# A spectral filter and a gated MLP on one core: the forward 47-point stage of the later batches with x stationary, and its result turned by transposing DMAs

## The chip, the core and the metric

The kernel runs on 1 core of one Trainium2 chip. The metric is device time in microseconds (us), from launch to end. All engines of the core work at once on their own instruction queues and meet through semaphores: PE (TensorE, matmuls; PEld are its weight loads), DVE (VectorE), ACT (ScalarE), POOL (GpSimd) and SP (SyncE, which here only issues DMAs).

## The reference

```python
def _attn_ref(x, filt_r, filt_i):              # x: 8 batches x 3008 x 256
    X = np.fft.rfft(x, axis=1)
    F = (filt_r + 1j * filt_i)[None, :, :]     # 1505 x 256
    return np.fft.irfft(X * F, n=x.shape[1], axis=1)

def _moe_ref(x, w_in, w_out, beta):            # 24064 tokens, 256 -> 2048 -> 256
    h = x @ w_in
    g = h * (1.0 / (1.0 + np.exp(-beta * h)))
    return g @ w_out
```

The output of the first is reshaped to 8 * 3008 = 24064 tokens and goes into the second. Inputs and output are float32; the kernel multiplies in bfloat16.

## The kernel before, in words

**The transform.** 3008 = 47 * 64. A token's index in its batch is 32 p + j with p = 0..93 and j = 0..31, and p = 2 n1 + q. The forward transform has two stages. Stage 1 (`s1`) is a 47-point transform over n1: a contraction over the 94 values of p with the table `t1` of 94 x 96, whose 96 columns are 24 frequencies k1 x 2 parts (real, imaginary) x 2 values of q. Stage 2 (`s2`) contracts, for each k1, over the 128 values of (part, q, j) with the table `t2`. So between the stages the data has to turn: stage 1 gives (k1, part, q) per j, and stage 2 needs (part, q, j) on the partitions per k1. After stage 2 DVE multiplies by the filter (L603, L604, L607), POOL adds the halves (L608, `yh`), and two inverse stages follow: `s3` (L619) with `t3` and `s4` (L641) with `t4`, with a turn through DRAM (`d2`) between them. `s4` writes `y`, which has the 256 channels on the partitions.

**Batch 0** is done ahead of the main loop with everything on chip, in functions of its own (`s1_0`, `a0_turn` and so on); there stage 1 already has x stationary and its result is turned by PE. It is not touched.

**Batches 1 to 7** are done inside the main loop. The loop has 752 steps: 47 blocks of 512 tokens by 16 blocks of 128 hidden units. A step does two matmuls of 512 columns for the hidden layer (L782), the swish on ACT (L791), and, two steps later, four matmuls of 256 columns into the block's accumulators (L800). Every 16 steps a block is finished, DVE copies it from PSUM (`ost<-acc`, tile pool `ostp` with 2 buffers), and SP stores it (`out_block`, L759 and L761).

**The order is written by hand.** `at(s, fn, ...)` puts a piece of the transform of a later batch behind the hidden layer of step s. `first_step[b]` is 0, 80, 176, 272 and so on, some 96 steps a batch; in the code o is `first_step[b - 1]`, the step at which the tokens of batch b - 1 begin to enter the MLP; in the steps that follow, `s2`, `s3` and `s4` of batch b are done. `s23_steps` places `s2` and `s3`, `s4_steps` places `s4`, `s1_steps` places the 16 units of stage 1 of the next batch: for batch 2 at steps 54 to 76, for each batch b + 1 above at o + 7, o + 13, o + 23 and so on to o + 76. So batch 3 begins stage 1 at step 87. The planned steps:

```python
at(o + 80, a2_load, 2, g)         # batch 2, o = 0; batch 1 has o + 16
at(o + 82, a2_load, b + 1, g)     # batches 3 to 7
```

**Stage 1 before.** A unit `s1(b, i)` is one matmul (L573): `t1` is the stationary operand (96 columns), and x, two values of j by 256 channels, 512 columns, is the moving one. The result of 96 partitions x 512 is cast into a tile `a1` (pool `apool`, 4 buffers, one tile for each 8 values of j), by DVE, in batch 1 by ACT in 5 of 16 units. After four units `a1_store` (L356) stores the tile in the DRAM scratch `d1`. `a2_load` (L581) reads `d1` back in the turned order, in 4 groups of 6 frequencies, into `a2` tiles (pool `a2pool`, 5 buffers). The data of one batch, 1.5 MB, thus goes to DRAM and back.

PSUM tiles of all these pieces come from one pool, `fpsum`, of 3 buffers. x of the later batches is loaded by POOL's DMA queue in chunks of 8 values of j (`load_x`, pool `xpool` of 4 buffers); a chunk serves four units of `s1`. [...]

Of the kernel before, what the change touches and what calls it, by code (L numbers as in the profile page):

```python
# [10 lines left out]
P = 128  # L11
# [5 lines left out]
BF16 = mybir.dt.bfloat16  # L17
# [7 lines left out]
NK = 24  # L25
J = 32
KG = 6
JG = 8
# [8 lines left out]
def kernel(  # L37
# [10 lines left out]
    nc = tc.nc  # L48

    B, S, D = x.shape  # L50
# [5 lines left out]
    NDC = D // P  # L56
    NFB = FF // P
    NP = 2 * N1
    KP = 4 * NK
# [11 lines left out]
    tw = dict(reuse_waits="tile")  # L71
    dpool = ctx.enter_context(tc.tile_pool(name="dram_scratch", bufs=2, space=bass.MemoryType.DRAM))
# [20 lines left out]
    t1 = consts.tile([NP, KP], BF16, name="t1", tag="t1")  # L93
# [10 lines left out]
    xg = {}  # L104
    ys = {}
    st = {}

    def evac(dst, src, on_act, scale=None):
        if on_act:
            nc.scalar.activation(dst, src, ACT.Copy, scale=1.0 if scale is None else scale)  # L110
        elif scale is None:
            nc.vector.tensor_copy(dst, src)  # L112
        else:
            nc.vector.tensor_scalar_mul(dst, src, scale)  # L114
# [129 lines left out]
    MG = 4  # L244
# [100 lines left out]

    r_sq.close()

    def d_tiles(b):
        st["d1", b] = dpool.tile([NK, P, D], BF16, name="d1", tag="d1")
        st["d2", b] = dpool.tile([NK, P, D], BF16, name="d2", tag="d2")  # L350

    def a1_store(b, g):
        if g == 0:
            d_tiles(b)
        rows = st["d1", b].rearrange("k (a j) d -> (k a) j d", j=J)
        nc.sync.dma_start(rows[:, g * JG : (g + 1) * JG, :], st["a1", b][:])  # L356

    wst = ctx.enter_context(tc.tile_pool(name="wstage", bufs=2, **tw))
    zzpool = ctx.enter_context(tc.tile_pool(name="zzpool", bufs=4, **tw))
    WG = 4  # L360
# [169 lines left out]
    def tail_tile(i, shape, dt=F32):  # L530
        return pair[i].tile(shape, dt, name="pt", tag=f"pt{i}")
# [10 lines left out]
    for e in range(NDC):  # L542
        for h in range(2):
            ps = tail_tile(2 - e, [P, 4, P])
# [9 lines left out]
    r_sr.close()  # L554
    right.close()

    apool = ctx.enter_context(tc.tile_pool(name="apool", bufs=4, **tw))
    hpsum = ctx.enter_context(tc.tile_pool(name="hpsum", bufs=2, space=bass.MemoryType.PSUM, **tw))
    opsum = ctx.enter_context(tc.tile_pool(name="opsum", bufs=3, space=bass.MemoryType.PSUM, **tw))
    fpsum = ctx.enter_context(tc.tile_pool(name="fpsum", bufs=3, space=bass.MemoryType.PSUM, **tw))  # L560
# [5 lines left out]
    ostp = ctx.enter_context(tc.tile_pool(name="ostp", bufs=2, **tw))  # L566

    def s1(b, i, on_act):
        g, jj = divmod(2 * i, JG)
        if jj == 0:  # L570
            st["a1", b] = apool.tile([KP, JG, D], BF16, name="a1", tag="a1")
        ps = fpsum.tile([P, 512], F32, name="ps1", tag="f")
        nc.tensor.matmul(  # L573
            ps[:KP], lhsT=t1[:], rhs=xg[b, g][:NP, jj : jj + 2, :], start=True, stop=True
        )
        evac(st["a1", b][:, jj : jj + 2, :], ps[:KP], on_act)

    def a2_load(b, h):
        cols = st["d1", b].rearrange("k m d -> m k d")
        t = a2pool.tile([P, KG, D], BF16, name="a2", tag="a2")  # L580
        nc.sync.dma_start(t[:], cols[:, h * KG : (h + 1) * KG, :])  # L581
        st["a2", b, h] = t

    def s2_matmuls(b, i):
# [25 lines left out]

    def s3(b, i, on_act):
        g, kk = divmod(2 * i, KG)
        if ("z", b, g) not in st:
            st["z", b, g] = [zpool.tile([P, KG, D], BF16, name="z", tag="z"), 0]
        z = st["z", b, g]
        yh = st.pop(("yh", b, i))
        ps = fpsum.tile([P, 2, D], F32, name="ps3", tag="f")
        for e in range(2):
            nc.tensor.matmul(  # L619
                ps[:, e, :], lhsT=t3[:, 2 * i + e, :P], rhs=yh[:, e, :], start=True, stop=True  # L620
            )
        evac(z[0][:, kk : kk + 2, :], ps[:], on_act)
        z[1] += 2
        if z[1] == KG:
            cols = st["d2", b].rearrange("k m d -> m k d")
            nc.sync.dma_start(cols[:, g * KG : (g + 1) * KG, :], z[0][:])
# [36 lines left out]
    def at(s, fn, *a):  # L663
        plan.setdefault(int(s), []).append((fn, a))

    def s1_steps(b, units_, steps, act, on_act=()):
        assert len(steps) == len(units_)
        for i, s in zip(units_, steps):
            at(s, s1, b, i, i in on_act)
            if i % 4 == 3:  # L670
                at(s, a1_store, b, i // 4)

    def s23_steps(b, steps, lag, act):
        assert len(steps) == NU
        for i, s in enumerate(steps):
            at(s, s2, b, i)
            at(s + lag, s3, b, i, i % act == act - 1 if act else False)
# [6 lines left out]
    for b in range(1, B):  # L684
        o = first_step[b - 1]
        if b == 1:
            at(0, z_late, 1, 0)
            at(1, z_late, 1, 1)
            s1_steps(1, range(16), [3 + (2 * i + 1) // 3 for i in range(16)], False, (1, 4, 7, 10, 13))
            for i, r in enumerate((2, 3, 4, 5)):  # L690
                at(r, f_late, 1, i // 2, i % 2)
            for g in range(NG):
                at(o + 16, a2_load, 1, g)
# [12 lines left out]
            if B > 2:  # L706
                for g in range(4):
                    at(o + 24 + 3 * g, load_x, 2, g)
                late = (54, 55, 56, 57, 58, 59, 60, 61, 66, 67, 68, 70, 72, 73, 74, 76)
                s1_steps(2, range(16), [o + r for r in late], False)  # L710
                for g in range(NG):
                    at(o + 80, a2_load, 2, g)
                if B > 3:
                    for g in range(4):
                        at(o + (62, 68, 88, 92)[g], load_x, 3, g)
# [8 lines left out]
        if b + 1 < B:  # L724
            early = [o + 16 * n + s for n in range(4) for s in (7, 13)]
            late = [o + s for s in (66, 67, 69, 70, 72, 73, 75, 76)]
            s1_steps(b + 1, range(16), early + late, False)
            for g in range(NG):
                at(o + 82, a2_load, b + 1, g)
            if b + 2 < B:  # L730
                for g in range(4):
                    at(o + (30, 62, 88, 92)[g], load_x, b + 2, g)
# [6 lines left out]
    for s in range(NSTEP):  # L739
        i, fb = divmod(s, NFB)  # L740
# [31 lines left out]
    for s in range(NSTEP + 4):  # L772
        if s < NSTEP:
            i, fb = divmod(s, NFB)
# [3 lines left out]
            while pos < t0 + TB:  # L778
                b, n0 = divmod(pos, S)
                ln = min(S - n0, t0 + TB - pos)  # L780
                for dc in range(NDC):
                    nc.tensor.matmul(  # L782
                        hps[:, pos - t0 : pos - t0 + ln],
                        lhsT=win_sb[:, dc, fb * P : (fb + 1) * P],
                        rhs=ys[b][:, dc, n0 : n0 + ln],
                        start=(dc == 0),
                        stop=(dc == NDC - 1),
# [10 lines left out]
        for i, fb, tb in outs.get(s, ()):  # L798
# [3 lines left out]
                lhsT=blk[i * NFB + fb][:, tb * P : (tb + 1) * P],  # L802
                rhs=wout_sb[:, fb, :],
                start=(fb == 0 and (tb % 2 == 0 or lone)),
                stop=(fb == NFB - 1),
# [35 lines left out]
```

## Time and profile before

| | |
|---|---|
| Median of 3 runs | 780.7 us (780.31 to 780.71) |
| Profiled execution: its time, its span | 780.71 us, 778.9 us |
| Busy: PE, ACT, DVE, POOL | 768.9, 552.7, 447.1, 150.9 us |
| Granted TensorE clock | 1.00 |
| Stores of a1 to d1 (L356) | 28 of 384 KB, 5.4 us from issue to landing |
| Loads of a2 from d1 (L581) | 28 of 384 KB, 5.2 us |
| Stage 1 matmuls (L573) | 112, 41.9 us busy |
| DVE casts of stage 1 | 107, 686 ns each |
| ACT casts of stage 1 | 5, 581 ns each |

How to read it: the span is the time from the first to the last instruction of one profiled execution, and its own time is 1.8 us above the span. Matmuls overlap, so that the mean duration of one contains its latency; what one costs in a stream is read from the distance of two starts. Lines such as L573 are lines of the kernel before; in the changed kernel the same lines of code have other numbers.

### The profile page before, as it was taken

Reading aid. Unit: us, or ns where it says so; the run is one execution under the profiler, and the core shown is the slowest. Engines: PE = TensorE matmul, PEld = TensorE weight load, DVE = VectorE, ACT = ScalarE, POOL = GpSimd, SP = SyncE. Lnnn points to the kernel's source line nnn. Section 1 sums busy time; section 2 is a strip of 40 time slices with the busy share of each in tenths; the row PEclk is TensorE's granted clock in tenths of the full one; section 3 lists DMA queues with packets and bytes.
Section 4 is the critical chain, followed back from the end, with each engine's and each line's share of the span. In section 5 each row is a group of like instructions: output and inputs, shape, how many; then the busy total and the mean of one; then the engine's idle time right before and its main releaser. Section 6 shows DMA issues by size and latency. Waiting matters only on the chain.

```text
span 778.9 us, 15241 instructions
## 1 busy us (share of the span) xinstructions
PE 768.9 (99%) x6048; PEld 543.7 (70%) x6048; DVE 447.1 (57%) x716; ACT 552.7 (71%) x813; POOL 150.9 (19%) x154
## 2 busy tenths in 40 slices
PE   8899999999999999999999999999999999999997
PEld 5667667666776667866678666776667766676665
DVE  8878754766556665566546665567655666321001
ACT  7767877666677766777667776677666777777776
POOL 6714300312012210122201322022200222000000
PEclk9999999999999999999999999999999999999999
DMA  9967485244813358042671417622164111500101
GB/s 201 210 194 165 135 216 149 74 109 112 244 48 84 100 123 235 29 114 70 152 207 45 120 48 179 179 75 68 49 189 134 50 48 48 157 28 28 55 28 55
DMA packets 84411, 88.71 MB, mean 114 GB/s; under 512 B 5788, under 2 KB 74652, under 8 KB 84340
## 3 DMA queue, kind: packets, MB, share of 16 engines
q1 hardware_dynamic: 77940, 74.20, 31.5%
q0 software_dynamic: 4192, 13.40, 10.5%
q8 instruction: 47, 0.77, 0.4%
q10 hardware_dynamic: 2208, 0.14, 0.2%
q14 instruction: 24, 0.20, 0.1%
HBM read 54.47 MB, written 46.66 MB: 130 GB/s over the span
## 4 chain that ended last, share of the span: by engine, by line
PE 96%; ACT 1%; DVE 1%; issue 0%; POOL 0%; DVEq 0%; POOLq 0%
PE acc L800 42%; PE hps L782 42%; PE ps L573 3%; PE ps L641 2%; PE ps L589 2%; PE ps L619 2%; PE sps L454 0%; PE tp L403 0%; ACT aT L110 0%; ACT t L110 0%; ACT y L110 0%; DVE pq_t L440 0%; PE ps L408 0%; DVE u L226 0%; PE sps L433 0%
## 5 line engine op out<-in xcount | busy, mean ns | idle before, releaser
L791 ACT ACTIVATE gT<-hps,beta_sb 128x512 bf16<-128x512 f32 x752 | 516.6, 687 | 213.7 <-PE hps L782 212.9
L800 PE MATMUL acc<-wout_sb,gT 128*128 128x256 bf16 x3008 | 453.1, 272 | 0.0
L782 PE MATMUL hps<-y,win_sb 128*128 128x512 bf16 (+7 forms) x1728 | 447.8, 351 | 0.1
L800 PEld LDWEIGHTS <-gT 128*128 128x128 bf16 x3008 | 286.7, 98 | 121.7 <-issue 1.2
L608 POOL TENSOR_TENSOR yh<-a_t,b_t 128x512 bf16<-128x512 f32 x84 | 106.4, 1267 | 422.5 <-DVE b_t L607 422.1
L782 PEld LDWEIGHTS <-win_sb 128*128 128x128 bf16 x1728 | 164.7, 98 | 24.4 <-DVE y L114 0.3
L112 DVE COPY ost<-acc 128x512 f32<-128x512 f32 (+1 forms) x94 | 60.0, 679 | 138.2 <-PE acc L800 138.2
L112 DVE CAST a<-ps 96x512 bf16<-96x512 f32 x107 | 73.0, 686 | 52.2 <-PE ps L573 51.4
L114 DVE TENSOR_SCALAR y<-ps 128x376 bf16<-128x376 f32 (+2 forms) x128 | 63.2, 509 | 61.5 <-PE ps L641 57.9
L603 DVE TENSOR_TENSOR a_t<-ps,fr_sb 128x512 f32<-128x512 f32 x84 | 58.1, 692 | 67.5 <-PE ps L589 67.0
L604 DVE SCALAR_TENSOR_TENSOR b_t<-ps,fi_sb 64x512 f32<-64x512 f32 x84 | 58.2, 693 | 1.1
L607 DVE TENSOR_TENSOR b_t<-ps,fi_sb 64x512 f32<-64x512 f32 x84 | 57.4, 684 | 1.1
L112 DVE CAST z<-ps 128x512 bf16<-128x512 f32 x72 | 49.3, 685 | 1.7 <-PE ps L619 0.8
L641 PEld LDWEIGHTS <-zz 96*128 96x128 bf16 x448 | 29.7, 97 | 22.9
L573 PE MATMUL ps<-xg,t 94*96 94x512 bf16 x112 | 41.9, 381 | 0.0
L641 PE MATMUL ps<-t,zz 96*128 96x94 bf16 x448 | 34.7, 205 | 0.0
L589 PE MATMUL ps<-a,t 128*128 128x256 bf16 x168 | 32.1, 273 | 0.0
L619 PE MATMUL ps<-yh,t 128*128 128x256 bf16 x168 | 32.1, 273 | 0.0
L619 PEld LDWEIGHTS <-t 128*128 128x128 bf16 x168 | 16.2, 98 | 17.7 <-issue 0.6
L589 PEld LDWEIGHTS <-t 128*128 128x128 bf16 x168 | 16.1, 98 | 16.1
L171 POOL DMA_DIRECT2D xg<-in_x_dram x24 | 12.5, 524 | 56.7 <-PE ps L573 56.7
L573 PEld LDWEIGHTS <-t 94*96 94x96 bf16 x112 | 13.8, 123 | 10.4
(95 smaller groups left out, 177.8 us busy)
## 6 DMA issues: line engine op xcount, KB each, us to landing
out_dram<-ost SPq DMA_DIRECT2D x42, 512.0 KB, 3.0
d<-a SPq DMA_DIRECT2D x28, 384.0 KB, 5.4
a<-d SPq DMA_DIRECT2D x28, 384.0 KB, 5.2
d<-z SPq DMA_DIRECT2D x28, 384.0 KB, 3.7
zz<-d SPq DMA_DIRECT2D x28, 384.0 KB, 6.9
xg<-in_x_dram POOLq DMA_DIRECT2D x24, 384.0 KB, 6.1
out_dram<-ost SPq DMA_DIRECT2D x9, 256.0 KB, 5.5
ws<-in_moe_w_out_dram SPq DMA_DIRECT2D x4, 512.0 KB, 8.9
```

The lines of the kernel that those rows point to most:

```text
L112: nc.vector.tensor_copy(dst, src)
L114: nc.vector.tensor_scalar_mul(dst, src, scale)
L573: nc.tensor.matmul(ps[:KP], lhsT=t1[:], rhs=xg[b, g][:NP, jj : jj + 2, :], start=True, stop=True)
L589: nc.tensor.matmul(ps[:, e, :], lhsT=t2[:, k0 + e, :], rhs=st["a2", b, g][:, kk + e, :], start=True, stop=True,)
L603: nc.vector.tensor_tensor(a_t[:], ps[:], fr_sb[:, ks, :], ALU.mult)
L604: nc.vector.scalar_tensor_tensor(b_t[:M], ps[M:], -1.0, fi_sb[M:, ks, :], ALU.mult, ALU.mult)
L608: nc.gpsimd.tensor_tensor(yh[:], a_t[:], b_t[:], ALU.add)
L619: nc.tensor.matmul(ps[:, e, :], lhsT=t3[:, 2 * i + e, :P], rhs=yh[:, e, :], start=True, stop=True)
L641: nc.tensor.matmul(ps[:, e, :NP], lhsT=zz[:, j0 % JG + e, dc * P : (dc + 1) * P], rhs=t4[:], start=True, stop=True,)
L782: nc.tensor.matmul(hps[:, pos - t0 : pos - t0 + ln], lhsT=win_sb[:, dc, fb * P : (fb + 1) * P], rhs=ys[b][:, dc, n0 : n0 + ln], start=(dc ...
L791: nc.scalar.activation(gT[:], hps[:], ACT.Silu, scale=beta_sb[:, fb : fb + 1])
L800: nc.tensor.matmul(acc_of(i, tb)[:, tb % 2, :], lhsT=blk[i * NFB + fb][:, tb * P : (tb + 1) * P], rhs=wout_sb[:, fb, :], start=(fb == 0 an ...
```

## The change

For batches 1 to 7, stage 1 takes x as the stationary operand. A unit has four matmuls, one for each of four values of j: the stationary operand is x of 94 values of p by 128 channels, the moving one is `t1` with 96 columns. The result has 128 channels on the partitions and 4 x 96 columns, and its cast, still on the same engine and at the same step, writes it with permuted columns into one tile `a1` for the whole batch, of 128 partitions by 2 (channel halves) x 96 x 32. `apool` has 1 buffer. There are still 16 units: 8 groups of j by 2 channel halves.

`a1_store` and the scratch `d1` are gone. `a2_load` issues, in each of its 4 groups, two transposing DMAs on SP (8 a batch), each of which takes 128 partitions by 768 columns (6 frequencies x 4 x 32) of `a1` and writes 6 blocks of 128 x 128, transposed, into the same `a2` tile as before. The steps at which the units and `a2_load` stand are unchanged. The scratch `d2` of the inverse turn stays; its allocation moves into `s3`. Stage 2 and all that follows are as before.

```diff
--- before.py
+++ after.py
@@ -345,16 +345,6 @@
 
     r_sq.close()
 
-    def d_tiles(b):
-        st["d1", b] = dpool.tile([NK, P, D], BF16, name="d1", tag="d1")
-        st["d2", b] = dpool.tile([NK, P, D], BF16, name="d2", tag="d2")
-
-    def a1_store(b, g):
-        if g == 0:
-            d_tiles(b)
-        rows = st["d1", b].rearrange("k (a j) d -> (k a) j d", j=J)
-        nc.sync.dma_start(rows[:, g * JG : (g + 1) * JG, :], st["a1", b][:])
-
     wst = ctx.enter_context(tc.tile_pool(name="wstage", bufs=2, **tw))
     zzpool = ctx.enter_context(tc.tile_pool(name="zzpool", bufs=4, **tw))
     WG = 4
@@ -554,7 +544,7 @@
     r_sr.close()
     right.close()
 
-    apool = ctx.enter_context(tc.tile_pool(name="apool", bufs=4, **tw))
+    apool = ctx.enter_context(tc.tile_pool(name="apool", bufs=1, **tw))
     hpsum = ctx.enter_context(tc.tile_pool(name="hpsum", bufs=2, space=bass.MemoryType.PSUM, **tw))
     opsum = ctx.enter_context(tc.tile_pool(name="opsum", bufs=3, space=bass.MemoryType.PSUM, **tw))
     fpsum = ctx.enter_context(tc.tile_pool(name="fpsum", bufs=3, space=bass.MemoryType.PSUM, **tw))
@@ -566,19 +556,32 @@
     ostp = ctx.enter_context(tc.tile_pool(name="ostp", bufs=2, **tw))
 
     def s1(b, i, on_act):
-        g, jj = divmod(2 * i, JG)
-        if jj == 0:
-            st["a1", b] = apool.tile([KP, JG, D], BF16, name="a1", tag="a1")
+        jq, e = divmod(i, NDC)
+        if i == 0:
+            st["a1", b] = apool.tile([P, NDC, KP, J], BF16, name="a1", tag="a1")
         ps = fpsum.tile([P, 512], F32, name="ps1", tag="f")
-        nc.tensor.matmul(
-            ps[:KP], lhsT=t1[:], rhs=xg[b, g][:NP, jj : jj + 2, :], start=True, stop=True
-        )
-        evac(st["a1", b][:, jj : jj + 2, :], ps[:KP], on_act)
+        g, m0 = divmod(jq * MG, JG)
+        for m in range(MG):
+            nc.tensor.matmul(
+                ps[:, m * KP : (m + 1) * KP],
+                lhsT=xg[b, g][:NP, m0 + m, e * P : (e + 1) * P],
+                rhs=t1[:],
+                start=True,
+                stop=True,
+            )
+        evac(
+            st["a1", b][:, e, :, jq * MG : (jq + 1) * MG],
+            ps[:, : MG * KP].rearrange("p (m k) -> p k m", k=KP),
+            on_act,
+        )
 
     def a2_load(b, h):
-        cols = st["d1", b].rearrange("k m d -> m k d")
         t = a2pool.tile([P, KG, D], BF16, name="a2", tag="a2")
-        nc.sync.dma_start(t[:], cols[:, h * KG : (h + 1) * KG, :])
+        for e in range(NDC):
+            nc.sync.dma_start_transpose(
+                t[:, :, e * P : (e + 1) * P],
+                st["a1", b][:, e, 4 * KG * h : 4 * KG * (h + 1), :].rearrange("p k j -> p (k j)"),
+            )
         st["a2", b, h] = t
 
     def s2_matmuls(b, i):
@@ -610,6 +613,8 @@
 
     def s3(b, i, on_act):
         g, kk = divmod(2 * i, KG)
+        if i == 0:
+            st["d2", b] = dpool.tile([NK, P, D], BF16, name="d2", tag="d2")
         if ("z", b, g) not in st:
             st["z", b, g] = [zpool.tile([P, KG, D], BF16, name="z", tag="z"), 0]
         z = st["z", b, g]
@@ -667,8 +672,6 @@
         assert len(steps) == len(units_)
         for i, s in zip(units_, steps):
             at(s, s1, b, i, i in on_act)
-            if i % 4 == 3:
-                at(s, a1_store, b, i // 4)
 
     def s23_steps(b, steps, lag, act):
         assert len(steps) == NU
```

## The prediction

> **What bounds the kernel now.** First the page's busy times, then the chain of work that ended last: both name TensorE.
>
> ```profile
> PE 768.9 (99%) x6048; PEld 543.7 (70%) x6048; DVE 447.1 (57%) x716; ACT 552.7 (71%) x813; POOL 150.9 (19%) x154
> ...
> PE 96%; ACT 1%; DVE 1%; issue 0%; POOL 0%; DVEq 0%; POOLq 0%
> PE acc L800 42%; PE hps L782 42%; PE ps L573 3%; PE ps L641 2%; PE ps L589 2%; PE ps L619 2%; PE sps L454 0%; PE tp L403 0%; ACT aT L110 0%; ACT t L110 0%; ACT y L110 0%; DVE pq_t L440 0%; PE ps L408 0%; DVE u L226 0%; PE sps L433 0%
> ```
>
> The reader is to see that TensorE (PE) never waits once the loop runs, so two things move the time: columns taken off PE, and any wait that newly stops it. L573 is the stage that changes. Next the groups by shape (operation, shapes, count, busy us, mean ns).
>
> ```profile
> L112 DVE CAST a<-ps 96x512 bf16<-96x512 f32 x107 | 73.0, 686 | 52.2 <-PE ps L573 51.4
> ...
> L114 DVE TENSOR_SCALAR y<-ps 128x376 bf16<-128x376 f32 x104 | 55.9, 547 | 58.1 <-PE ps L641 57.9
> ...
> L573 PE MATMUL ps<-xg,t 94*96 94x512 bf16 x112 | 41.9, 381 | 0.0
> L641 PE MATMUL ps<-t,zz 96*128 96x94 bf16 x448 | 34.7, 205 | 0.0
> ```
>
> L641, the inverse 47-point stage, already has the form that L573 gets: data stationary, four matmuls of 94 columns into one bank, then an eviction of 128x(94x4) with the same strides. It is the template for the new stage. A mean of one matmul contains its latency, so the price is read from start to start in PE's timeline.
>
> ```profile
> 106.31 0.50 PE L641 MATMUL ps<-t,zz 96*128 96x94 bf16 x8
> 106.64 0.39 PE L573 MATMUL ps<-xg,t 94*96 94x512 bf16 x1
> 106.86 0.60 PE L800 MATMUL acc<-wout_sb,gT 128*128 128x256 bf16 x4
> ```
>
> Eight 94-column matmuls take 106.64 - 106.31 = 0.33 us, 41.3 ns each, with their weight loads hidden. One 512-column matmul takes 0.22 us; the step's pairs of 512 columns take 0.435, so 0.2175 us.
>
> Last the places where the removed round trip and the next batch meet, in batch 2, on DVE and then on SP's queue.
>
> ```profile
> 119.31 0.69 DVE L112 CAST a<-ps 96x512 bf16<-96x512 f32 x1 [0.71 <-PE ps L573]
> ...
> 129.55 0.69 DVE L112 CAST a<-ps 96x512 bf16<-96x512 f32 x1 [4.03 <-PE ps L573]
> 130.71 0.69 DVE L603 TENSOR_TENSOR a_t<-ps,fr_sb 128x512 f32<-128x512 f32 x1 [0.48 <-PE ps L589]
> ```
>
> ```profile
> 120.03 0.32 SPq L356 DMA_DIRECT2D d<-a  x1
> 123.06 2.37 SPq L581 DMA_DIRECT2D a<-d  x4
> 125.54 15.53 SPq L761 DMA_DIRECT2D out_dram<-ost  x2
> ```
>
> The last cast of batch 2's stage ends at 120.00; the first cast of batch 3's stage starts at 129.55. With four a1 tiles nothing connects them. With one tile the second has to wait for everything that reads the first.
>
> [...]
>
> **The change part by part.**
>
> PE: 112 units lose 1 matmul of 512 columns and gain 4 of 96. New unit: 4 x 41.3 x 96/94 = 168.7 ns. Saved: (217.5 - 168.7) x 112 = 5.4 us, all on the path, since PE is the path.
>
> Evictions: the casts of 686 ns become about 547 (the L114 row), 0.14 us less each, 15 us on DVE in all. DVE is at 57%; worth nothing except where a cast is late.
>
> DMA: 28 stores and 28 loads of 384 KB go, 56 transposes of 192 KB come (8 a batch, 128 partitions by 768 columns). The old wait of the load for the stores goes; its 5.4 + 5.2 us landings were hidden, as PE shows no wait for `a`. SP issues 8 transposes where it issued 4 stores and 4 loads. What queues behind them on SP are output and z stores; the next output store, ready at 125.5, goes late. `ost` has two buffers and the one after next is wanted a block (15 us) later still, so this costs nothing unless SP is held for some 25 us. POOL's queue is untouched: the x chunks are freed after the same units.
>
> The new wait: with apool at one buffer, the first cast of batch b+1 waits until all 8 transposes of batch b have landed. The changed program's first such cast in each batch carries waits on the DMA semaphores. Behind it on DVE stand the filter products of the running batch (L603 to L607), which feed POOL's add and then PE's L619.
>
> Let T be the time from the start of the 8 transposes to the landing of the last. Batch 2 has the short deadline. The transposes can start at 120.0. The cast is due at 129.55. It may slip by 0.48 (DVE's idle before a_t), by 0.14 (its own shortening) and by the slack further down:
>
> ```profile
> 132.95 1.27 POOL L608 TENSOR_TENSOR yh<-a_t,b_t 128x512 bf16<-128x512 f32 x1 [20.15 <-DVE b_t L607]
> ```
>
> ```profile
> 136.13 0.38 PE L619 MATMUL ps<-yh,t 128*128 128x256 bf16 x2
> ```
>
> 136.13 - 134.22 = 1.91. So PE stops when the cast starts after 132.08, that is, T above **12.1 us**. The other consumers are later: the first pair of transposes feeds L589 at 130.22, and PSUM's third buffer of the stage runs out at 135.03.
>
> Batches 3 to 6 are looser. In batch 3 the output store ahead on SP is issued by 205.15, and the cast of batch 4 is due at 224.99, with slack 0.48 + 0.14 + (231.78 - 229.65 = 2.13): T above **22.6 us**. Their later equals have the same pitch. Batch 1 has until 94.6 us for its reuse, and its first group must land 9.9 us after the last cast; batch 7 has no successor. Neither binds below T = 39.
>
> T from both sides. [...] I take 22.4, since [...]nothing shows that these overlap. An estimate[...].
>
> Stop in batch 2: 22.4 - 12.1 = 10.3 us. [...] Batches 3 to 6: nothing, just below 22.6.
>
> Sum: 778.9 - 5.4 + 10.3 + 1.7 = 785.5 us of span. The profiled execution took 780.71 with that span, 1.8 around it, and the median is 780.7: **787.3 us**.
>
> **The rivals.**
>
> *All covered.* T up to 12.1: [...]only PE's columns count: 780.7 - 5.4 = 775.3. For it: [...]a plain load's issue is 0.6 us of SP (2.37 / 4). [...] This ends faster; it decides from T = 12.1 down, and the change stays a gain until the stop of batch 2 eats 3.8 of the 5.4 us, T = 15.9.
>
> *Every batch stops.* T above 22.6: one a1 tile makes each batch wait for the transposes of the one before. At T = 34: batch 2 loses 21.9 + 1.7, batches 3 to 6 each 11.4 + 1.7, in all 76.0: 851.3. [...]
>
> *Weight loads show.* Were four loads of 97 ns (L641's weight-load row) not hidden, a unit would take 0.39 us, +0.17 x 112 = 19 us: 800. Against it stands the 41.3 ns of L641.
>
> *Not as said:* excluded, since the changed program has 56 transposes on SP and no first scratch store.
>
> **How the numbers follow.** All covered: 0.27. Batch 2 alone stops: 0.38 (T below 15.9, faster: 0.10; T to 18, within 0.2%: 0.07; above, slower: 0.21). Every batch stops: 0.32. Weight loads: 0.03. So faster 0.37, same 0.07, slower 0.56; 0.2%, 1.6 us, is about what a measurement of this kernel can tell from no change. The likeliest case alone spans 775 to 789. The range: low 774.5, high 851, which leaves out T above 34, about 0.15, and little below.
>
> **What would show it.** Right: 448 matmuls at the old L573 with start distances of 41 to 43 ns; casts of 128x384 near 550 ns; one DVE wait for a DMA ahead of the first such cast, near 130 us, and one PE gap of about 10 us near 136. [...] Wrong: no DVE wait for the transposes (all covered, T was small), or a wait of that kind in every batch and PE idle about 95 us apart (T was large); or a PE unit of 0.3 us and more.

## The result, and the profile after

The changed kernel takes 776.5 us (776.16 to 776.85, 4 runs) against 780.6 us; the ratio is 0.9948, with an interval of 0.9931 to 0.9965. It is faster by 4.1 us. The forecast was 787.3 us, slower; 776.5 is close to the rival that has every transpose covered (775.3).

First the page of the changed kernel: busy times, the chain of work that ended last by engine, and the stage's groups (the cast on DVE, the matmuls on PE).

```profile
PE 763.8 (99%) x6384; PEld 550.2 (71%) x6384; DVE 433.0 (56%) x716; ACT 552.2 (71%) x813; POOL 151.0 (20%) x154
...
PE 94%; DMA 2%; ACT 1%; DVE 1%; POOL 1%; issue 0%; DVEq 0%; POOLq 0%
...
L112 DVE CAST a<-ps 128x384 bf16<-128x384 f32 x107 | 59.1, 556 | 58.0 <-PE ps L565 47.5
...
L565 PE MATMUL ps<-t,xg 94*128 94x96 bf16 x448 | 36.7, 205 | 0.0
```

TensorE (PE) is still busy for 99% of a span of 774.4 us. Its stage went from 41.9 to 36.7 us, which is the gain; the casts went from 686 to 556 ns. New in the chain are 2% of DMA and 1% of POOL, where the page of before has no DMA and 0% of POOL: the page puts the DMA share down to the load of the output weights (`ws`), and POOL scales these weights. They come up again below.

PE's timeline gives the price of a unit. Here two units, eight matmuls, run from 40.92 to the start of the next group.

```profile
40.92 0.51 PE L565 MATMUL ps<-t,xg 94*128 94x96 bf16 x8
41.26 0.61 PE L393 MATMUL tp<-ident,y 128*128 128x128 bf16 x8
```

Eight matmuls take 0.34 us, 42.5 ns each, in this pair of starts; a unit costs 0.170 us where it cost 0.2175, and 112 units save 5.3 us. The profiled spans differ by 4.5.

Now the new wait: SP's queue and DVE at the end of batch 2. `x8` is eight transposes merged into one row.

```profile
116.99 12.21 SPq L581 DMA_TRANSPOSE a<-a  x8
```

```profile
118.54 0.56 DVE L112 CAST a<-ps 128x384 bf16<-128x384 f32 x1 [0.66 <-PE ps L565]
...
130.94 0.56 DVE L112 CAST a<-ps 128x384 bf16<-128x384 f32 x1 [6.20 <-DMA a<-a]
131.53 0.69 DVE L606 TENSOR_TENSOR a_t<-ps,fr_sb 128x512 f32<-128x512 f32 x1
```

The wait is there, once, at the forecast place: DVE stands still for 6.2 us until the eighth transpose has landed. What it costs is read from POOL's add and PE's next consumer.

```profile
133.77 1.27 POOL L611 TENSOR_TENSOR yh<-a_t,b_t 128x512 bf16<-128x512 f32 x1 [21.56 <-DVE b_t L610]
```

```profile
135.24 0.38 PE L624 MATMUL ps<-yh,t 128*128 128x256 bf16 x2
```

`yh` is ready at 133.77 + 1.27 = 135.04, and PE comes to it at 135.24. No time is lost, by 0.2 us. The prediction's limit counts from the end of the last cast, where it lets the transposes begin. From there (118.54 + 0.56 = 119.10) to the released cast (130.94) T is 11.8 us, against a limit of 12.1.

The transposes did not all begin there. The first of the eight reads one channel half alone, which was complete one unit earlier: it was issued at 116.99, took 1.25 us, and the second followed at 119.12, just after the last cast. So seven of the eight were left when the prediction's count begins. Had all eight been left, T would be about 13.1 us, over the limit by 1 us (an estimate: 11.8 and one median issue of 1.29; no run takes this head start away).

The output store behind the transposes on SP, whose copy ended at 124.74, was issued at 129.30, late as forecast, and nothing waited for it.

The transposes themselves, from the view of the tile: count, duration of the issue on SP in ns (min/median/max), first and last start, and the time from issue to landing.

```profile
L581 SPq DMA_TRANSPOSE a<-a x56: 1211/1287/2614, 50.6 to 591.8; - x56
...
DMA to landing us min/median/max: 2.7/2.8/5.4
```

Last, a wait that has nothing to do with the transposes. PE at step 10, changed kernel:

```profile
46.32 0.51 PE L565 MATMUL ps<-t,xg 94*128 94x96 bf16 x8
47.55 0.60 PE L803 MATMUL acc<-wout_sb,gT 128*128 128x256 bf16 x4 [0.73 <-POOL wout_sb L367]
```

PE reaches the third group of output weights before POOL has scaled them. The same place in the kernel before:

```profile
46.79 0.60 PE L573 MATMUL ps<-xg,t 94*96 94x512 bf16 x2
47.40 0.60 PE L800 MATMUL acc<-wout_sb,gT 128*128 128x256 bf16 x4
```

Here 0.61 us pass for 0.435 us of columns, so 0.18 us of wait was there already. The 0.56 us that PE has gained by then (46.32 + 0.34 against 46.79 + 0.435) is given back, and 0.15 us more, since L803 starts at 47.55 and L800 did at 47.40. That closes the sum: 5.3 - 0.7 = 4.6 us, against 4.5 in the spans.

### The profile page after: what moved, and what is told of

It is laid out like the page before. It is cut to its first block, busy times and chain, and to the rows that moved or that the text cites. A ratio compares the mean times of both kernels' runs of the same rounds, so it can differ in the third digit from the quotient of the medians.

```text
span 774.4 us, 15904 instructions
## 1 busy us (share of the span) xinstructions
PE 763.8 (99%) x6384; PEld 550.2 (71%) x6384; DVE 433.0 (56%) x716; ACT 552.2 (71%) x813; POOL 151.0 (20%) x154
## 4 chain that ended last, share of the span: by engine, by line
PE 94%; DMA 2%; ACT 1%; DVE 1%; POOL 1%; issue 0%; DVEq 0%; POOLq 0%
PE acc L803 42%; PE hps L785 41%; PE ps L646 2%; PE ps L592 2%; PE ps L624 2%; PE ps L565 2%; DMA ws<-in_moe_w_out_dram 2%; POOL wout_sb L367 0%; PE sps L444 0%; ACT aT L110 0%; ACT t L110 0%; ACT y L110 0%; DVE u L226 0%; POOL xg L171 0%; PE sps L423 0%
## 5 line engine op out<-in xcount | busy, mean ns | idle before, releaser
L803 PE MATMUL acc<-wout_sb,gT 128*128 128x256 bf16 x3008 | 453.2, 272 | 0.7 <-POOL wout_sb L367 0.7
L803 PEld LDWEIGHTS <-gT 128*128 128x128 bf16 x3008 | 281.1, 98 | 102.9 <-issue 1.8
L112 DVE CAST a<-ps 128x384 bf16<-128x384 f32 x107 | 59.1, 556 | 58.0 <-PE ps L565 47.5
L565 PEld LDWEIGHTS <-xg 94*128 94x128 bf16 x448 | 30.4, 97 | 19.9
L565 PE MATMUL ps<-t,xg 94*128 94x96 bf16 x448 | 36.7, 205 | 0.0
L624 PE MATMUL ps<-yh,t 128*128 128x256 bf16 x168 | 32.1, 273 | 0.0
L624 PEld LDWEIGHTS <-t 128*128 128x128 bf16 x168 | 16.2, 98 | 17.7 <-issue 0.6
```

The lines of the kernel that those rows point to most:

```text
L565: nc.tensor.matmul(ps[:, m * KP : (m + 1) * KP], lhsT=xg[b, g][:NP, m0 + m, e * P : (e + 1) * P], rhs=t1[:], start=True, stop=True,)
L624: nc.tensor.matmul(ps[:, e, :], lhsT=t3[:, 2 * i + e, :P], rhs=yh[:, e, :], start=True, stop=True)
L803: nc.tensor.matmul(acc_of(i, tb)[:, tb % 2, :], lhsT=blk[i * NFB + fb][:, tb * P : (tb + 1) * P], rhs=wout_sb[:, fb, :], start=(fb == 0 an ...
```

## The experiments

Two theories. **Columns**: the gain is PE's columns, 5.2 to 5.3 us, and what is missing of it was lost at the output weights, while the transposes stay inside their slack. **Wait**: the wait of batch 2 costs the missing part. Separate from both is the question why T was 11.8 and not 22.4. Each run changes the changed kernel; of the edits the main lines are shown, with notes behind `#` where lines are left out.

### The changed kernel again

> The changed kernel once more, as the yardstick for its neighbours. Theory (fewer columns on TensorE, transposes hidden, about 0.7 us given back to a wait for the output weights near 47 us): about 776.5, 4.1 us under the kernel before, and in the profile one VectorE wait for the transposes near 131 us of about 6 us without a TensorE gap behind it. Rival (the wait for the output weights is an accident of one execution): no TensorE wait near 47 us in this profile.

Measured: 776.28 us (775.84 to 777.39), ratio 0.9943 (0.9931 to 0.9956). Its profile has the same wait for the output weights:

```profile
47.56 0.60 PE L803 MATMUL acc<-wout_sb,gT 128*128 128x256 bf16 x4 [0.74 <-POOL wout_sb L367]
```

So that wait is no accident of one execution. The cast of batch 3 starts at 130.85 after 6.10 us of idle DVE, and PE's L624 at 135.24 again.

### A third staging tile for the output weights

```diff
-    wst = ctx.enter_context(tc.tile_pool(name="wstage", bufs=2, **tw))
+    wst = ctx.enter_context(tc.tile_pool(name="wstage", bufs=3, **tw))
```

> Staging tiles for the output weights 3 in place of 2, so that the third load need not wait for the first scaling on GpSimd. Theory (0.7 us of the gain is lost to that wait): the third scaling starts before 40 us, the TensorE wait near 47 us is gone, 0.7 us faster than the changed kernel, about 775.8. Rival (the missing part of the gain lies in the matmuls themselves or in the batch-2 wait): same time as the changed kernel, 776.5.

Measured: 776.64 us (776.24 to 777.84), 0.9945 (0.9933 to 0.9958): the same as the changed kernel, a miss. PE's timeline shows why.

```profile
38.58 0.60 PE L785 MATMUL hps<-y,win_sb 128*128 128x512 bf16 x2 [0.71 <-DMA win_sb<-in_moe_w_in_dram]
...
135.68 0.38 PE L624 MATMUL ps<-yh,t 128*128 128x256 bf16 x2 [0.48 <-POOL yh L611]
```

The wait at 47 us is gone, but the third weight load, now issued earlier, runs beside the load of `win_sb`, whose 768 KB land in 9.8 us where they took 8.5; PE waits 0.71 us for them. And in this execution the eight transposes took 12.98 us of issue instead of 12.21, the cast started at 131.53, and batch 2 stopped PE for 0.48 us. The gain met other waits. The second line is also the first sight of the limit from the other side.

### The third scaling in halves

```diff
+        n = WG // 2 if f0 == 2 * WG else WG
+        for f in range(f0, f0 + WG, n):
-        nc.gpsimd.tensor_tensor(...)   # WG blocks
+            nc.gpsimd.tensor_tensor(...)   # n blocks
```

> The third scaling of the output weights on GpSimd is split into two halves, so that the first half is ready some 0.9 us earlier; no DMA moves. Theory (0.7 us of the gain is lost to that wait): the TensorE wait near 47 us is gone and nothing takes its place, 0.7 us under the changed kernel, about 775.6. Rival (whatever is gained there meets the next wait, as with the third staging tile): 776.3.

Measured: 775.71 us (775.54 to 776.6), 0.9937 (0.9923 to 0.995). PE at step 10:

```profile
46.37 0.51 PE L568 MATMUL ps<-t,xg 94*128 94x96 bf16 x8
46.71 0.60 PE L806 MATMUL acc<-wout_sb,gT 128*128 128x256 bf16 x4
```

The matmul with the output weights follows after 0.34 us, with no wait. The 0.6 us that this brings against the changed kernel is the size of the wait, and its span, 773.6, is 0.8 under. The columns theory holds; the difference of the medians is no larger than the spread of single runs, and the wait that has gone from the timeline is the better evidence.

### Batch 3's first unit four steps later

```diff
             early = [o + 16 * n + s for n in range(4) for s in (7, 13)]
+            if b == 2:
+                early[0] = o + 11
```

> The first unit of batch 3's changed stage moves from step 87 to step 91, so its cast comes due some 4 us later, after the filter products of batch 2 that stood behind it. Theory (the VectorE wait for the transposes in batch 2 stays just inside its slack, 0.2 us in the profiled execution, and is passed only in executions whose transposes are slower): the VectorE wait of 6 us is gone, the time is the changed kernel's within 0.4 us, 776.0 to 776.4. Rival (that wait costs what is missing of the gain): 775.4 or less.

Measured: 776.4 us (775.54 to 776.68), 0.994 (0.9928 to 0.9953). The 6 us wait on DVE is gone, and the time is the changed kernel's.

```profile
129.91 0.69 DVE L606 TENSOR_TENSOR a_t<-ps,fr_sb 128x512 f32<-128x512 f32 x1 [4.96 <-PE ps L592]
...
132.63 0.56 DVE L112 CAST a<-ps 128x384 bf16<-128x384 f32 x1 [0.63 <-PE ps L565]
```

The wait theory, which asked for 775.4 or less, falls: a wait of 6.2 us on DVE cost nothing that these runs can tell.

### Both edits

> The two edits together: scaling in halves, and the first unit of batch 3 at step 91. Theory: neither wait is left, the whole 5.2 us of TensorE columns shows: 775.3 to 775.6, and a smaller spread. Rival: as each alone, 776.3.

Measured: 775.35 us (775.12 to 776.84), 0.9934 (0.9921 to 0.9946). The middle is as forecast; the spread is not smaller.

### A fifth matmul in each unit

```diff
-        for m in range(MG):
+        for m in (*range(MG), 0):
```

> Each unit of the changed stage does a fifth matmul (it repeats its first one, same result): 112 more of 96 columns with their weight loads. Theory (a matmul costs its columns, loads hidden, all on the path): 42 ns each, +4.7 us against the changed kernel, about 781.2, which gives back the whole gain. Rival (weight loads show in part, or the stage hides under something else): +10.9 us at 97 ns each, or nothing.

Measured: 781.8 us (781.3 to 782.9, 13 runs), 1.0012 (1.0004 to 1.002): 5.5 us above the changed kernel and above the kernel before. By shape:

```profile
L565 PE MATMUL ps<-t,xg 94*128 94x96 bf16 x560 | 41.5, 205 | 1.3
```

The stage's busy time rose from 36.7 to 41.5 us, 4.8 for 112 matmuls, 43 ns each, so the weight loads of 97 ns are hidden. The 0.7 us left is about what a wait can explain, for this kernel is past the limit as well:

```profile
137.94 0.38 PE L624 MATMUL ps<-yh,t 128*128 128x256 bf16 x2 [1.10 <-POOL yh L611]
```

### Every transpose twice

```diff
+            nc.sync.dma_start_transpose(
+                dumpool.tile([P, KG, P], BF16, name="dum", tag="dum")[:],
+                st["a1", b][:, e, 4 * KG * h : 4 * KG * (h + 1), :].rearrange("p k j -> p (k j)"),
+            )                                                   # dumpool: a new pool, 2 buffers
```

> Each transpose is issued a second time into a dummy tile, so the one a1 tile is held about twice as long. Theory (TensorE stops once the first cast of the next batch starts later than about 2.5 us after its due time; issue on SP at some 1.3 to 1.5 us each sets the pace): the last transpose of batch 2 lands near 141 us, a TensorE gap of about 10 us near 136 us and some 2 us in each of batches 3 to 6[...]: about 796, between 790 and 805. Rival (the wait has far more slack than reckoned): under 779.

Measured: 807.16 us (805.39 to 810.55), 1.0343 (1.0321 to 1.0365): 31 us above the changed kernel, more than the 20 expected. From the waits (in all, times, longest) and from DVE's and PE's timelines:

```profile
DVE a L112 <- DMA dum<-a: 34.6, 4, 17.0
...
PE ps L566 <- DVE a L112: 8.0, 1, 8.0
...
PE ps L597 <- DMA a<-a: 3.2, 1, 3.2
```

```profile
147.86 0.56 DVE L112 CAST a<-ps 128x384 bf16<-128x384 f32 x1 [17.01 <-DMA dum<-a]
```

```profile
148.47 0.48 PE L566 MATMUL ps<-t,xg 94*128 94x96 bf16 x4 [8.01 <-DVE a L112]
```

The mechanism that the prediction described is real: once the last transpose lands late, the one `a1` tile stops DVE, and PE behind it. Two things were under-reckoned. Batch 1 stops too, 3.2 us for its own transposes: PE goes on at 84.67, 34.6 us after the first of them was issued at 50.11, while the prediction let batch 1 bind from T = 39 on. And the clock: the stage table (length, busy us of PE, PEld, DVE, ACT and POOL, granted clock, DMA share, GB/s) gives

```profile
140.00:148.50 8.50, 0.49 (x6) 0.25 (x4) 0.61 (x2) 0.84 (x2) 0.00 (x0) 0.80 0.89 162
148.50:156.00 7.50, 6.10 (x31) 3.81 (x32) 5.24 (x8) 1.51 (x3) 3.01 (x3) 0.54 0.39 70
```

a clock of 0.54 for 7.5 us after the stop. That is 7.5 x 0.46 = 3.4 us, or 2.8 on the 6.10 us in which PE was busy (estimates), and not the 1.7 that the prediction's sum allows. From 34 to 130 us, where the stop of batch 1 lies, the mean granted clock is 0.96, where the changed kernel has 1.00: on 90.8 us of busy PE some 3.6 us more (an estimate). PE's new waits for these stages come to some 21 us (8.0, 3.2, and 9.9 in eleven short ones); with the clock after the two stops that is some 27 of the 30.5 us by which the profiled span grew. The rest is open.

### The size of a transpose: halved, then doubled

```diff
-                t[:, :, e * P : (e + 1) * P],                       # 768 columns
+                t[:, 3 * n : 3 * n + 3, e * P : (e + 1) * P],       # n = 0, 1: 384 columns each
```

> Each transpose is split into two of 384 columns [...], same data, same place. Theory [...]: issue 0.64 to 0.75 us each, the 8 transposes of a batch still done in about 12 us, time 776 to 777. Rival [...]: issue 0.9 to 1.2 us, batch 2's transposes land 4 us and more later and TensorE stops there: 779 to 781.

Measured: 798.39 us (796.24 and 800.55, 2 runs), 1.0225 (1.0197 to 1.0252), far above both forecasts.

```profile
L583 SPq DMA_TRANSPOSE a<-a x112: 1177/1255/2422, 50.2 to 626.9; - x112
...
DMA to landing us min/median/max: 2.3/2.4/8.8
```

Half the columns, nearly the same issue: 1.255 against 1.287 us. Sixteen take 22.34 us of SP at the end of batch 2, and PE stops there for 6.91 us, to 145.41. Up to 154.44 PE is slow: a group of four matmuls of 256 columns takes 0.83 to 0.86 us from start to start, against 0.435 before the stop (the mean granted clock of the whole execution is 0.989). So the price does not go with the columns: the theory's 0.64 is about half of 1.287, and the issue is above the rival's 1.2 as well.

A second path adds to the time. In batch 1 the sixteen hold SP for 22.37 us, to 72.56; two output stores follow, issued at 62.70 in the changed kernel, and then a store of `z`, issued at 73.95. ACT waits 3.6 us for it to land, and PE 2.75 us behind ACT; PE goes on at 86.07, 12.1 us after the issue of a store whose kind lands after 3.8 us (median). The prediction saw no cost in what queues behind the transposes unless SP is held for some 25 us. Why this store landed so late is not tested.

Then the double size, in four transposes:

```diff
-        t = a2pool.tile([P, KG, D], BF16, name="a2", tag="a2")
+        t = a2pool.tile([P, 2 * KG, D], BF16, name="a2", tag="a2")   # a2pool: 3 buffers
-                st["a1", b][:, e, 4 * KG * h : 4 * KG * (h + 1), :]
+                st["a1", b][:, e, 4 * KG * h : 4 * KG * (h + 2), :]   # h = 0, 2
```

> Four transposes a batch of 1536 columns [...] in place of eight of 768; the a2 tiles hold 12 frequencies, 3 buffers. Halving the size left the issue at 1.25 us. Theory P (SP pays by the instruction, about 1.25 us whatever the size): issue 1.3 us each, four in 6 us, landing 4 to 6 us after the issue; batch 2's last lands near 125 us, before the cast is due, and the VectorE wait for the transposes is gone. Theory T (a floor of 1.25 us[...]): issue 2.56 us each, a batch still takes 11 to 12 us and the VectorE wait stays. Time in both: 776.0 to 776.5, since the wait is inside its slack.

Measured: 776.2 us (775.46 to 776.4), 0.9939 (0.9925 to 0.9952).

```profile
L583 SPq DMA_TRANSPOSE a<-a x28: 1481/1963/3327, 50.8 to 588.4; - x28
...
DMA to landing us min/median/max: 3.8/4.6/6.5
```

```profile
117.19 8.08 SPq L583 DMA_TRANSPOSE a<-a  x4
```

```profile
128.91 0.56 DVE L112 CAST a<-ps 128x384 bf16<-128x384 f32 x1 [3.97 <-PE ps L565]
```

1.96 us each: neither 1.3 nor 2.56, which is about twice the 1.287 of 768 columns. Four are issued in 8.08 us where eight took 12.21 (both with the wait for the last cast behind the first transpose), and the cast waits for PE only. Neither of the two theories was right: of the three sizes tried, 384 and 768 columns cost 1.25 to 1.29 us, and 1536 columns 0.7 us more. What sets that, SP's own work or the data behind it, these runs do not separate. The time is again that of the changed kernel, as it must be if the wait was covered.

### Double size, and scaling in halves

> Four transposes of 1536 columns and the third scaling in halves, first unit of batch 3 at step 87 as in the changed kernel. Theory P: no DMA wait on VectorE, no wait for the output weights, 775.3. Theory T: 775.3 to 775.7, with the wait on VectorE left.

Measured: 775.3 us (774.83 to 775.79), 0.9929 (0.9917 to 0.9941), with no DMA wait on DVE and none for the output weights on PE. It is the lowest of all, 1.2 us under the changed kernel's first median, and it is not tied to an edge of 0.2 us.

## Why the prediction was wrong

**The direction failed on one term, the time of a batch's transposes.** The step is "T from both sides", with "I take 22.4". That was the author's estimate: the trace of before holds no transposing DMA, so it showed no price for one. Measured, T is 11.8. Three things were wrong in it.

- 22.4 us allow 2.8 us for each of the eight, with the landing of the last in it. An issue took 1.29 us (median).
- The transposes overlap. Eight issues took 12.21 us together, with a wait of 0.88 us for the last cast among them, while each landed 2.8 us (median) after its own issue. That nothing showed an overlap was no argument for none.
- One transpose was under way before the count began, worth about 1.3 us. This was read from the trace; no run tried it alone.

That PE did not stop at all hung on little. Without the early transpose T would be about 13.1, which is past the limit and would cost about 1 us; the change would still be faster, since by the prediction's own sum the gain lasts until T = 15.9.

**The limit was right.** It was 12.1 us for batch 2. Four profiles of the same eight transposes lie on both sides of it; T counts from the end of the last cast to the released cast.

| Run | T, us | At PE's next use of `yh` |
|---|---|---|
| the changed kernel | 11.8 | ready 0.20 us early |
| scaling in halves | 12.1 | ready 0.05 us early |
| third staging tile | 12.6 | PE stops 0.48 us |
| fifth matmul | 13.4 | PE stops 1.10 us |

Each row puts the limit between 12.0 and 12.3. Where the wait would stand (one DVE wait, near 130 us) was right; only PE behind it did not stop. A forecast whose direction hung on T being above or below some 16 us should not have rested on one value of T that no trace showed.

**PE's columns were right:** 5.4 us forecast (its sum gives 5.5); 5.3 us from the starts in the timeline, 5.2 from the busy times, and the fifth matmul costs 43 ns. The rival in which the weight loads show is out by the same figures.

**The rival "all covered" had the mechanism in the main, and missed by 1.2 us** (775.3 against 776.5). It asked that a batch's transposes stay under the limit, as they did, since an issue took 1.29 us and one of the eight had an early start. Most of the 1.2 us is the wait for the output weights: PE sped up ahead of a deadline on POOL that it had only just passed before. Without that wait, the medians are 775.3 to 775.7. The casts' 0.13 us each and the removed round trip brought nothing that the sum leaves room for, as forecast.

**The clock's price after a stop was too low.** The 1.7 us in the prediction's sum were the author's estimate; the clock of before is 1.00. After the stop of 8.0 us the trace shows 0.54 for 7.5 us: 3.4 us over the whole stretch, or 2.8 on the time in which PE was busy (estimates). After the stop of 6.91 us the eight groups of L805 and L787 took some 0.85 us each in place of 0.435: 3.3 us in all (an estimate). In the changed kernel there was no stop, and its clock is 1.00.

## What to carry to other kernels

When a removed buffer makes one stage wait for transfers of another, work out the slack down to the bounding engine's next use, and then ask on which side of it the transfers end: here a wait of 6.2 us on an engine with slack cost nothing, and the transposes 0.8 us later stopped PE for 0.48 us. Count from where each transfer can really start; the first may not need the last piece of data. An engine that gets faster meets the deadlines of others earlier, so look for the last thing that just came in time before; here a scaling on POOL took back 0.6 us, and splitting it gave that back without moving a DMA. Where the issue of a DMA costs nearly the same at two sizes, as here at 384 and 768 columns, fewer and larger ones free the queue sooner: four in place of eight took SP 8.08 us in place of 12.21. Here that bought a margin and no time.

## What the runs showed of the hardware

- A transposing DMA from SBUF to SBUF held SP for 1.25 us (median) at 384 columns of 128 partitions, 1.29 us at 768 and 1.96 us at 1536, and landed 2.4, 2.8 and 4.6 us after its issue. At 768 and 1536 columns, 197 and 393 KB, the issue alone allows 153 and 200 GB/s. Seven of a batch's eight, 1.38 MB, took 11.8 us from the issue of the first of them to the released cast: 117 GB/s.
- A stop of PE of 8.0 us was followed by 7.5 us at a mean granted clock of 0.54. One of 6.91 us was followed by 9.0 us in which a group of four matmuls of 256 columns took 0.83 to 0.86 us from start to start in place of 0.435, and the first such group after one of 2.75 us took 0.85 us. The profiled executions with stops of 0.48 and 1.10 us had a mean clock of 0.999.
- Matmuls of 96 columns with a new weight load each run at 42.5 ns from start to start, with a mean duration of 205 ns each; the loads of 97 ns are hidden.
